# An attention, mixture-of-experts and feed-forward kernel: the second item's expert by signed comparisons, five low parts on GpSimd, and the last tiles' choice between the last attention units

## The chip, the cores and the metric

The kernel runs on one core of one Trainium2 chip. The metric is the device time of one execution in microseconds (us). The kernel before was timed three times: median 835.39 us, from 835.25 to 836.21. Rows of the trace come from one further execution that was profiled; times in them count from the start of its span.

## The reference, cut

```python
# attention: 4 batches x 8 heads, 576 positions, 64 per head; causal window of 128; a slope per head
scores = where(mask, q @ k.T / sqrt(64) + bias, -1e9)
attn = softmax(scores) @ v                         # -> x, 2304 tokens x 512
# mixture of experts: 8 experts, one per token
logits = x @ w_gate + modality_bias[modality_id]
e_idx = argmax(logits, axis=1)
gate_w = softmax(logits)[e_idx]
for e in range(8):
    h = maximum(x[e_idx == e] @ w1[e], 0.0)        # 512 -> 1024
    out[e_idx == e] = gate_w * (h @ w2[e])         # 1024 -> 512
# feed-forward: 512 -> 2048 -> 512, weights in float64
h = out @ w_in
return (h * cos(h)) @ w_out
```

## The kernel before

**Precision.** Products that need all of float32 are made from two parts: a high part, which is the number cast to fp32r, and a low part, which is the number minus its high part. One product of weights and activations is then three matmuls: high by high, high by low, low by high. For a piece of expert weights the raw load lands in `r1` or `r2` (two buffers each, 128x1024 float32), ScalarE (ACT) makes the high part by a cast, and VectorE (DVE) the low part by a subtraction that reads the raw data and the high part. This is `split_w1` (L502) and `split_w2` (L1184). A raw buffer is free for the next load when the low part is done.

**Attention.** 18 tiles of 128 tokens, each in two halves of four heads, make 36 units. A unit n passes `tr` (transposes of q and k, split into parts), `score`, `flip` (transposes of the exponentials, through `pa` and `pT`) and `pv`, which writes its half of a tile `X[t]`; after the second half the tile is stored to `x_dram`. The two last tiles are called `y`.

**Routing.** `xt_split` transposes a finished tile into the two parts `xT`. For each pair of tiles `logits(t)` (L854) gives three calls: `products` (the gate's 8 matmuls and a copy `ls`), `choose` (transposes of `ls`, then 8 small DVE instructions from `lg` to the one-hots `oh` and `ohb`) and `ranks(t)` (L241). `ranks` makes counting products from `ohb`, the running `cum` and constants `tri` and `ones`; folds them into each token's rank in its expert; adds the pair to `cum`; and cuts the rank into blocks of 128 and a remainder, by `ri`, `ph`, `pf` and the one-hots `ob`.

**The order of experts.** Experts have 256 slots per item. The first item's expert is the fullest after the first 12 tiles (`early`, L265); its gathered rows and weights are asked for while the attention still runs. The other eight come from the counts of all 18 tiles (`late`, L320). `sums` turns the counts `rp` into numbers per expert: `K3` (full items, and halves that are over), their prefix sums `pre` over the order of experts `M`, and the block starts `pblk` and `endF`. `slots` makes each token's place as one-hots `oa`, `table` the index table `idx` by products on TensorE, and `experts`, held behind `oa`, the expert of each item: intervals of blocks, folded and cast to `regs`. `load_w1(i, 0)` (L226) reads item i's entry of `regs` on the SP queue and issues the load with it.

**Items.** Nine items of 8 steps each; step f is an up product (12 matmuls `bk<-xT,s`) of item i, and three steps later its down product (12 matmuls `bk<-hh,s`). Weights come in four pieces of W1 and four of W2 per item, W1(i, g) and W2(i, g). Split pieces live in the three tiles `s_0`, `s_1`, `s_2` for W1 (`s1s`) and two more, also printed as `s_0` and `s_1`, for W2 (`s2s`). The first item's up products 0 to 3 run within the attention stage, on two split pieces in a buffer of K that is no longer used (`s1k`, tile name `kT`). `hh` is the rectified result in two parts, made by ACT and DVE; the down sums are evicted to `y` by both. In the loop ACT and DVE also convert the feed-forward's float64 weights, a bit at a time (`from_f64`, L112: `mag`, `top`, `lf`, `wi_a`); the multiplication `lf` of 128x512 is GpSimd's (POOL), and the conversion's loads are on SP between the weight loads.

**What sets the order.** Instructions are put in order by a scheduler, except where a chain is made: `issue_after` puts an instruction behind another on its engine. `Turns` (L523) does so for all instructions of an engine while it is on (for TensorE and POOL nearly all of the attention stage, for ACT and DVE its final sequence: program order there); `InOrder` does the same in steps 12 to 66. `behind("act", "dve")` holds the splits of the first two steps behind marks of the last `xt_split`. The gathers of rows are issued by POOL, the other loads and the stores by SP, in the order of the program's queues.

The final sequence of the attention stage is at L980 to L1017: scores of units 34 and 35, splits of W1(0, 0) and W1(0, 1), `xt_split` of tiles 15, 16 and 17, the calls of `last14` (tiles 14 and 15) and `last16` (16 and 17), and `up_products(0, 0)` to `(0, 3)` between. Its last lines are

```python
        up_products(0, 2)
        last16[1]()
        up_products(0, 3)
        for eng in (nc.scalar, nc.vector, nc.gpsimd, nc.tensor):
            eng.on = False
        after = last16[2:]
```

and what stands in `after`, `ranks(T - 2)`, `sums`, `slots`, `table` and `experts`, is taken up in the loop over steps, one or two calls a step.

Of the kernel before, what the change touches and what calls it, by code (L numbers as in the profile page):

```python
# [29 lines left out]
def kernel(  # L30
# [174 lines left out]
    regs = rt.tile([1, 2 * NL + 2], I32, name="regs")  # L205
    xTs = [rt.tile([128, 2, KD, SLOTS], F32R, name=f"xT{j}") for j in range(2)]
# [15 lines left out]
    W1, HH = {}, {}  # L222
    E = {}
# [17 lines left out]
    def ranks(t):  # L241
# [8 lines left out]
        fold(rank[:, t:t + 2], rp[:, 0:2], oh[:, t:t + 2], [128, 2, NE], rt)  # L250
        if t == 0:
            V_.tensor_tensor(cum, oh[:, 0], oh[:, 1], op=ALU.add)
        elif t + 2 < T:
            V_.tensor_tensor(cum, cum, oh[:, t], op=ALU.add)
            V_.tensor_tensor(cum, cum, oh[:, t + 1], op=ALU.add)
        ri = rt.tile([128, 2], I32, name="ri")
# [5 lines left out]
        one_hot(ob[:, t:t + 2], 128, pf[:, 1, t:t + 2], 2)  # L262

# [56 lines left out]
    def late():  # L320
# [3 lines left out]
        A3 = rt.tile([128, 3, NE], F32, name="A3")  # L324
        a3 = rt.tile([128, 3, T], F32, name="a3")
        pidx = rt.tile([128, NE], F32, name="pidx")
        pblk = rt.tile([128, NE], F32, name="pblk")
        endF = rt.tile([128, NE], F32, name="endF")
# [4 lines left out]
        def sums():  # L333
# [20 lines left out]
            V_.tensor_scalar(A3[:, 0], pre[:, 0], 2.0, None, op0=ALU.mult)  # L354
            V_.tensor_scalar(A3[:, 1], K3[:, 0], 2.0, None, op0=ALU.mult)
            V_.tensor_tensor(endF, A3[:, 0], A3[:, 1], op=ALU.add)
            V_.tensor_tensor(A3[:, 2], pblk, endF, op=ALU.subtract)
            E["m9"] = m9

        def experts():  # L360
# [4 lines left out]
            nb = rt.tile([1, NE], F32, name="nb")  # L365
            V_.scalar_tensor_tensor(nb, K3[0:1, 1], 2.0, K3[0:1, 2], op0=ALU.mult, op1=ALU.add)
            V_.tensor_tensor(nb, nb, pblk[0:1], op=ALU.add)
            b = rt.tile(shp, F32, name="b_", tag="fold3")
            inF = rt.tile(shp, F32, name="inF")
            V_.tensor_tensor(inF, bl, rowp(A3[:, 0]), op=ALU.is_ge)  # L370
# [13 lines left out]
        def slots():  # L384
# [9 lines left out]
            MK["oa"] = V_.tensor_tensor(oa, oa, row.unsqueeze(2).to_broadcast([128, T, NBLK]), op=ALU.mult)  # L394
# [11 lines left out]
        def starts():  # L406
# [15 lines left out]
            V_.scalar_tensor_tensor(dq, A3[:, 2], 128.0, dq, op0=ALU.mult, op1=ALU.add)  # L422
# [15 lines left out]
        def rows_of():  # L438
# [3 lines left out]
            V_.scalar_tensor_tensor(dt, a3[:, 0], 128.0, dt, op0=ALU.mult, op1=ALU.add)  # L442
# [46 lines left out]
    def to_xT(i, j, now=True):  # L489
# [6 lines left out]
        def parts():  # L496
            nc.scalar.copy(xT[:, 0, :, cs], pt)
            nc.vector.tensor_tensor(xT[:, 1, :, cs], pt, xT[:, 0, :, cs].bitcast(F32), op=ALU.subtract)

        return parts() if now else parts  # L500

    def split_w1(i, g, s1=None):  # L502
# [4 lines left out]
        def low():  # L507
            nc.vector.tensor_tensor(s1[:, 1], r1, s1[:, 0].bitcast(F32), op=ALU.subtract)
# [3 lines left out]
    def up_products(i, f):  # L512
        g, j = divmod(f, 2)
        w, xT = W1[i, g], xTs[i % 2]
        if j == 0:
            HH[i, g] = bank("S", [128, 2, SLOTS])
        ph = HH[i, g]
        for kk in range(KD):
# [29 lines left out]
    with ExitStack() as c:  # L548
# [8 lines left out]

        MARK = {}
# [84 lines left out]
        def setup_tables():  # L643
# [35 lines left out]
            return turns + [middle]  # L679
# [164 lines left out]
        def xt_split(t):  # L844
# [9 lines left out]
        def logits(t):  # L854
# [3 lines left out]
            def products():  # L858
                pl = bank("L", [2 * NE, 256])
                for a in range(2):  # L860
                    for kk in range(KD):
                        nc.tensor.matmul(pl, wg[:, kk].rearrange("p a e -> p (a e)"), xT[:, a, kk],
                                         start=kk == 0 and a == 0, stop=kk == KD - 1 and a == 1)
# [676 lines left out]
```

## Time and profile before

| | |
|---|---|
| median of three timed runs | 835.39 us |
| the profiled execution: its own time, its span | 838.82 us, 837.1 us |
| mean granted TensorE clock of it | 0.985 |
| busy: TensorE matmul (PE), weight load (PEld) | 800.7 us (96%), 705.9 us (84%) |
| busy: VectorE (DVE), ScalarE (ACT), GpSimd (POOL) | 615.8 us (74%), 492.2 us (59%), 197.8 us (24%) |

An instruction group in the trace has its line, engine and operation, then what it writes and reads by the program's names; buffer numbers are left out, so that `s` stands for all split pieces and `r` for all raw ones. L535 is the one line on which `Turns` issues, so all of the attention stage and the routing has it; L1168 is that of `InOrder`, for the items and what follows. A bracket at the end of a row gives how long the engine was idle before it and what ended that. The down products of the first item begin at 187.6 us, the nine items and the unit behind them end at some 430 us, and the feed-forward fills the rest.

### The profile page before, as it was taken

Reading aid. Unit: us, or ns where it says so; the run is one execution under the profiler, and the core shown is the slowest. Engines: PE = TensorE matmul, PEld = TensorE weight load, DVE = VectorE, ACT = ScalarE, POOL = GpSimd, SP = SyncE. Lnnn points to the kernel's source line nnn. Section 1 sums busy time; section 2 is a strip of 40 time slices with the busy share of each in tenths; the row PEclk is TensorE's granted clock in tenths of the full one; section 3 lists DMA queues with packets and bytes.
Section 4 is the critical chain, followed back from the end, with each engine's and each line's share of the span. In section 5 each row is a group of like instructions: output and inputs, shape, how many; then the busy total and the mean of one; then the engine's idle time right before and its main releaser. Section 6 shows DMA issues by size and latency. Waiting matters only on the chain. (4 is left out here: it accounts for less than half of the span.)

```text
span 837.1 us, 14764 instructions
## 1 busy us (share of the span) xinstructions
PE 800.7 (96%) x5278; PEld 705.9 (84%) x5278; DVE 615.8 (74%) x1472; ACT 492.2 (59%) x912; POOL 197.8 (24%) x256
## 2 busy tenths in 40 slices
PE   8999999997999999999999999999999999999996
PEld 5888988887989999999978788787788888888995
DVE  4777786778899999995749999896665555555562
ACT  6775776562667766664637676754544555444562
POOL 4755664511022222330001221212222001100100
PEclk9999999999899999999999999999999999999998
DMA  9754531352788889778433231501311001100000
GB/s 165 164 141 117 137 95 33 127 190 87 261 281 265 272 259 301 246 234 310 155 107 96 82 117 60 177 25 64 100 56 58 1 1 38 38 1 1 26 26 25
DMA packets 125134, 103.40 MB, mean 124 GB/s; under 512 B 61725, under 2 KB 105027, under 8 KB 125059
## 3 DMA queue, kind: packets, MB, share of 16 engines
q1 hardware_dynamic: 121043, 92.48, 37.0%
q0 software_dynamic: 2960, 9.70, 3.4%
q8 instruction: 42, 0.69, 0.3%
q10 hardware_dynamic: 1056, 0.26, 0.2%
q14 instruction: 33, 0.27, 0.1%
HBM read 85.90 MB, written 16.52 MB: 122 GB/s over the span
## 5 line engine op out<-in xcount | busy, mean ns | idle before, releaser
L1168 PE MATMUL bk<-hh,s 128*128 128x256 f32 x864 | 118.3, 286 | 6.5 <-DVE y L1168 3.5
L1168 PEld LDWEIGHTS bk<-hh,s 128*128 128x128 f32 x864 | 109.4, 192 | 8.0 <-DVE y L1168 4.3
L1168 PE MATMUL bk<-xT,s 128*128 128x256 f32 x816 | 112.4, 288 | 3.9 <-ACT s L1168 3.5
L1168 POOL TENSOR_TENSOR lf<-lf,mag 128x512 f32<-128x512 f32 x32 | 47.2, 1474 | 287.1 <-DVE mag L1168 261.9
L1168 PEld LDWEIGHTS bk<-xT,s 128*128 128x128 f32 x816 | 105.3, 196 | 4.5 <-ACT s L1168 3.7
L1168 PE MATMUL bk<-yT,wi_a 128*128 128x512 f32 (+1 forms) x480 | 104.1, 368 | 1.2 <-DVE yT L1168 0.8
L1168 PE MATMUL bk<-yT,wi_b 128*128 128x512 f32 (+1 forms) x480 | 104.8, 367 | 0.0
L1168 ACT CAST s<-r 128x1024 fp32r<-128x1024 f32 x70 | 73.0, 1049 | 52.7 <-DMA r<-in_moe_w_dram 33.9
L1168 DVE TENSOR_TENSOR s<-r,s 128x1024 fp32r<-128x1024 f32 x70 | 92.1, 1317 | 15.6 <-ACT s L1168 14.8
L1168 ACT ACTIVATE r<-r 128x512 f32<-128x512 f32 (+1 forms) x80 | 47.2, 590 | 93.6 <-DVE r L1168 93.6
L1168 PEld LDWEIGHTS bk<-yT,wi_a 128*128 128x128 f32 x480 | 83.7, 188 | 17.3 <-DVE yT L1168 1.1
L1168 PEld LDWEIGHTS bk<-yT,wi_b 128*128 128x128 f32 x480 | 84.4, 188 | 15.7
L1168 DVE TENSOR_TENSOR r<-bk,r 128x512 f32<-128x512 f32 (+1 forms) x80 | 51.0, 637 | 61.0 <-ACT r L1168 60.3
L1168 PE MATMUL bk<-wo_b,gg 128*128 128x512 f32 x384 | 93.4, 391 | 1.8 <-DVE po L1168 1.1
L1168 PE MATMUL bk<-wo_a,gg 128*128 128x512 f32 x384 | 92.7, 390 | 0.3 <-DVE gg L1168 0.2
L1168 PEld LDWEIGHTS bk<-wo_b,gg 128*128 128x128 f32 x384 | 71.5, 188 | 18.6 <-issue 1.3
L1168 PEld LDWEIGHTS bk<-wo_a,gg 128*128 128x128 f32 x384 | 71.9, 188 | 16.1 <-DVE gg L1168 1.2
L1168 DVE TENSOR_TENSOR gg<-r,gg 128x512 fp32r<-128x512 f32 x64 | 46.6, 728 | 34.4 <-ACT gg L1168 34.4
L535 PE MATMUL bk<-vt,pT 128*128 128x65 f32 x544 | 65.6, 273 | 0.2 <-POOL pT L535 0.2
L535 PEld LDWEIGHTS bk<-vt,pT 128*128 128x128 f32 x544 | 63.6, 192 | 1.8 <-issue 1.2
L1168 ACT CAST gg<-r 128x512 fp32r<-128x512 f32 x64 | 39.7, 620 | 41.0 <-DVE r L1168 40.9
L1168 DVE SCALAR_TENSOR_TENSOR r<-ki,bk 128x512 f32<-128x512 int32 (+1 forms) x80 | 50.4, 630 | 14.8 <-ACT ki L1168 14.2
(274 smaller groups left out, 1286.7 us busy)
## 6 DMA issues: line engine op xcount, KB each, us to landing
r<-in_moe_w_dram SPq DMA_DIRECT2D x72, 512.0 KB
y_dram<-y SPq DMA_DIRECT2D x19, 256.0 KB
rqk<-in_q_dram SPq DMA_DIRECT2D x32, 128.0 KB
vt<-in_v_dram SPq DMA_DIRECT2D x32, 128.0 KB
x_dram<-xt SPq DMA_DIRECT2D x16, 256.0 KB
f64x<-in_moe_w_in_dram SPq DMA_DIRECT2D x8, 512.0 KB
raw<-in_moe_w_dram SPq DMA_DIRECT2D x8, 512.0 KB
yg<-y_dram SPq DMA_DIRECT2D x16, 256.0 KB
```

The costliest lines, as they stand in the source:

```text
L535: self.last = op(*args, **kwargs)
L1168: r = op(*args, **kwargs)
```

## The change

It does four things.

1. **The second item's expert.** `sums` also computes `nb`, the block where an expert's odd half item ends, and from four borders per expert, compared with 2 and multiplied by constant signs, sums to the number of the expert that holds block 2. That number is cast to a register of its own, `reg1`, which `load_w1(1, 0)` reads. `signed` holds the signs times the expert's number, four small instructions in the attention stage. `A3`, `endF`, `pblk` and `nb` become rows of one tile `Q6`; `experts` still makes the others' entries.
2. **Low parts on GpSimd.** `split_w1` and `split_w2` take an engine. W2(0, 0), W1(0, 2), W2(0, 1), W1(0, 3) get their low part from GpSimd and live in spare buffers of K (`spare`), and W2(0, 2) gets its from GpSimd too, in the loop.
3. **The last four tiles' choice.** `ranks` is cut in `rank_counts` (TensorE), `rank_sums` and `rank_parts` (DVE). Choice and counts of tiles 14 and 15 go between the last attention units, `xt_split` of tiles 16 and 17 and the choice of these move ahead, and their counts stand before `up_products(0, 3)`.
4. **Loads of the first item.** W1(0, 2), W2(0, 1), W1(0, 3) and W2(0, 2) are asked for within the final sequence; in the loop W2 of the first item is asked for before W1 of the second. The loop's splits begin at W1(1, 0) and W2(0, 2), held behind marks of the sequence's last instructions on ACT, DVE and POOL while n is below 8.

```diff
...
     def load_w1(i, g):
         if g == 0:
             rg = 2 * NL + 1 if i == 0 else i
-            EV[i] = nc.sync.value_load(regs[0:1, rg:rg + 1], min_val=0, max_val=NE - 1)
+            EV[i] = nc.sync.value_load(reg1 if i == 1 else regs[0:1, rg:rg + 1], min_val=0, max_val=NE - 1)
...
-            V_.tensor_scalar(A3[:, 0], pre[:, 0], 2.0, None, op0=ALU.mult)
-            V_.tensor_scalar(A3[:, 1], K3[:, 0], 2.0, None, op0=ALU.mult)
-            V_.tensor_tensor(endF, A3[:, 0], A3[:, 1], op=ALU.add)
-            V_.tensor_tensor(A3[:, 2], pblk, endF, op=ALU.subtract)
+            V_.tensor_scalar(A3[:, 2], pre[:, 0], 2.0, None, op0=ALU.mult)
+            V_.tensor_scalar(A3[:, 0], K3[:, 0], 2.0, None, op0=ALU.mult)
+            V_.tensor_tensor(endF, A3[:, 2], A3[:, 0], op=ALU.add)
+            V_.scalar_tensor_tensor(nb, K3[:, 1], 2.0, K3[:, 2], op0=ALU.mult, op1=ALU.add)
+            V_.tensor_tensor(nb, nb, pblk, op=ALU.add)
+            at2 = rt.tile([1, 4, NE], F32, name="at2", tag="fold3")
+            V_.scalar_tensor_tensor(at2, Q6[0:1, 2:6], 2.0, signed, op0=ALU.is_le, op1=ALU.mult)
+            e1 = rt.tile([1, 1], F32, name="e1_")
+            V_.tensor_reduce(e1, at2, op=ALU.add, axis=AX.XY)
+            V_.tensor_copy(reg1, e1)
+            V_.tensor_tensor(A3[:, 1], pblk, endF, op=ALU.subtract)
...
+            def signs():
+                for j in range(4):
+                    nc.vector.tensor_scalar(signed[:, j], iota[0:1, 0:NE], -1.0 if j % 2 else 1.0, None, op0=ALU.mult)
...
-    def split_w1(i, g, s1=None):
+    def split_w1(i, g, s1=None, eng=None):
...
-            nc.vector.tensor_tensor(s1[:, 1], r1, s1[:, 0].bitcast(F32), op=ALU.subtract)
+            (eng or nc.vector).tensor_tensor(s1[:, 1], r1, s1[:, 0].bitcast(F32), op=ALU.subtract)
...
         run(flip(N - 4))
         low()
+        load_w1(0, 2)
+        load_w2(0, 1)
         xt_split(TX - 1)
         half = to_xT(0, 0, False)
         run(flip(N - 3))
         low = split_w1(0, 1, s1k[1])
+        home = spare()
+        split_w2(0, 0, as_w2(home[0]), nc.gpsimd)
         pv(N - 4)
         last14[0]()
         low()
-        half()
-        to_xT(0, 1)
+        load_w1(0, 3)
+        load_w2(0, 2)
+        halves = [half, to_xT(0, 1, False)]
+        halves = [h() for h in halves]
         run(flip(N - 2))
+        last14[1]()
         pv(N - 3)
+        rank_counts(TX - 2)
+        halves[0]()
         run(flip(N - 1))
         pv(N - 2)
-        pv(N - 1)
-        xt_split(T - 2)
-        last14[1]()
+        halves[1]()
+        split_w1(0, 2, as_w1(home[1]), nc.gpsimd)()
+        xt_split(T - 2, lambda: pv(N - 1))
+        xt_split(T - 1)
         up_products(0, 0)
-        xt_split(T - 1)
-        up_products(0, 1)
-        last14[2]()
-        last16[0]()
+        rank_sums(TX - 2)
+        rank_parts(TX - 2)
+        home = spare()
+        last16[0](lambda: split_w2(0, 1, as_w2(home[0]), nc.gpsimd))
+        up_products(0, 1, range(2))
+        last16[1]()
+        up_products(0, 1, range(2, KD))
+        split_w1(0, 3, as_w1(home[1]), nc.gpsimd)()
         up_products(0, 2)
-        last16[1]()
+        rank_counts(T - 2)
         up_products(0, 3)
+        MARK.update(act=nc.scalar.last, dve=nc.vector.last, pool=nc.gpsimd.last)
...
+        def after16():
+            rank_sums(T - 2)
+            rank_parts(T - 2)
+
+        after = [after16]
...
-        done_l = 2
-        done_s = [2, 0]
+        done_l = NF // 2
+        done_s = [NF // 2, 2]
...
-                        low = (split_w1, split_w2)[a](*pieces[done_s[a]])
+                        low = (split_w1, split_w2)[a](*pieces[done_s[a]], None, nc.gpsimd if done_s[a] == 2 else None)
...
         after.pop(0)()
-        with behind("act", "dve"):
-            splits(2, 1)
...
+                    if pieces[done_l - 1][0] == 0:
+                        load_w2(*pieces[done_l - 1])
                     if done_l < len(pieces):
                         load_w1(*pieces[done_l])
-                    if done_l:
+                    if pieces[done_l - 1][0]:
                         load_w2(*pieces[done_l - 1])
                     done_l += 1
-                if n == 1:
-                    splits(3, 2)
...
-                    with behind(*("act", "dve")[:2 if n < 2 else 0]):
+                    with behind("act", "dve", "pool") if n < NF else ExitStack():
                         splits((n + 1) // 2 + 3, n // 2 + 1)
...
```

On GpSimd, at the end of the attention stage, before (`pT` is made by the last attention units, `xg` are gathered rows):

```order
L535 AFFINE_SELECT pT<-pa 128x512 x4
L1168 DMA xg_99<-x_dram,idx 128x512
L1168 DMA xg_100<-x_dram,idx 128x512
L1168 DMA xg_99<-x_dram,idx 128x512
L1168 DMA xg_100<-x_dram,idx 128x512
```

and in the change, from the same place on (`kT` are the spare buffers of K with the first item's pieces, `s_0` is the tile of W2(0, 2)):

```order
L558 AFFINE_SELECT pT<-pa 128x512 x4
L558 TENSOR_TENSOR kT<-r_3124,kT 128x1024
L558 TENSOR_TENSOR kT<-r_3274,kT 128x1024
L558 TENSOR_TENSOR kT<-r_3276,kT 128x1024
L558 TENSOR_TENSOR kT<-r_3330,kT 128x1024
L1227 TENSOR_TENSOR s_0_3552<-r_3332,s_0_3552 128x1024
L1227 DMA xg_101<-x_dram,idx 128x512
```

Five subtractions of 128x1024 stand between the last `pT` and the first gather with the table `idx`.

On DVE, the sums of tiles 14 and 15 up to the first instruction of the choice of tiles 16 and 17, before:

```order
L535 TENSOR_TENSOR fold<-bk,oh 128x16
L1168 TENSOR_TENSOR s_0_3519<-r_3118,s_0_3519 128x1024
L535 TENSOR_REDUCE rank<-fold 128x2
L535 TENSOR_TENSOR cum<-cum,oh 128x8
L1168 TENSOR_TENSOR s_2_3518<-r_3563,s_2_3518 128x1024
L535 TENSOR_TENSOR cum<-cum,oh 128x8
L535 CAST ri<-rank 128x2
L1168 SCALAR_TENSOR_TENSOR hh<-bk,hh 128x512
L535 TENSOR_SCALAR ph<-ri 128x2 x2
L1168 TENSOR_TENSOR s_0_3516<-r_3605,s_0_3516 128x1024
L535 CAST pf<-ph 128x2x2
L535 TENSOR_TENSOR ob<-iota,pf 128x256
```

and in the change:

```order
L558 TENSOR_TENSOR fold<-bk,oh 128x16
L558 TENSOR_REDUCE rank<-fold 128x2
L558 TENSOR_TENSOR cum<-cum,oh 128x8 x2
L558 CAST ri<-rank 128x2
L558 TENSOR_SCALAR ph<-ri 128x2 x2
L558 CAST pf<-ph 128x2x2
L558 TENSOR_TENSOR ob<-iota,pf 128x256
L558 TENSOR_TENSOR lg<-bk,biasm 128x16
```

Three low parts and one `hh` no longer stand among the small instructions.

On TensorE, from the first item's up products to the counts of tiles 16 and 17, before (`xT_97,kT` is up with the pieces in K's buffer, `hh,s_0` is down, `xT_97,s_2` is up(0, 4); `tri` opens the counts):

```order
L535 MATMUL bk<-xT_98,wg 16x256 x8
L535 MATMUL bk<-xT_97,kT 128x256 x12
L535 MATMUL bk<-ident,ls 128x16 x2
L535 MATMUL bk<-xT_97,kT 128x256 x12
L1168 MATMUL bk<-hh,s_0_3519 128x256 x9
L1168 MATMUL bk<-xT_97,s_2_3518 128x256 x12
L1168 MATMUL bk<-hh,s_0_3519 128x256 x4
L1168 LDWEIGHTS tri
L1168 MATMUL bk<-ohb,tri 128x8
```

and in the change (`xT_99,kT` is up):

```order
L558 MATMUL bk<-xT_99,kT 128x256 x12
L558 MATMUL bk<-xT_100,wg 16x256 x8
L558 MATMUL bk<-xT_99,kT 128x256 x6
L558 MATMUL bk<-ident,ls 128x16 x2
L558 MATMUL bk<-xT_99,kT 128x256 x18
L558 LDWEIGHTS tri
L558 MATMUL bk<-ohb,tri 128x8
```

The counts stand 18 up products behind the transposes of `ls`, and up(0, 3) behind the counts.

## Rows read from the trace of the kernel before

**Rows 1.** Waits of TensorE from 170 us on: line, releaser, total us, times, longest.

```profile
PE bk L1168 <- ACT s L1168: 3.5, 1, 3.5
PE bk L1168 <- DVE y L1168: 3.5, 3, 1.4
...
PE bk L1168 <- DMA xg<-x_dram,idx: 1.6, 2, 0.8
...
PE bk L1168 <- DVE s L1168: 0.5, 1, 0.5
```

**Rows 2.** Timeline of TensorE, 185 to 218 us: start, us, instruction, xcount, [idle before <-releaser].

```profile
185.88 0.29 PE L535 MATMUL bk<-ident,ls 16*128 16x16 f32 x2
...
190.58 0.18 PE L1168 MATMUL bk<-ohb,tri 128*128 128x8 bf16 x1
...
209.74 0.79 PE L1168 MATMUL bk<-xT,s 128*128 128x256 f32 x2 [3.48 <-ACT s L1168]
...
215.48 1.58 PE L1168 MATMUL bk<-hh,s 128*128 128x256 f32 x12
216.90 1.60 PE L1168 MATMUL bk<-xT,s 128*128 128x256 f32 x12
```

**Rows 3.** Windows: us, PE PEld DVE ACT POOL busy (xcount), PEclk, DMA share, GB/s.

```profile
206.00:208.00 2.00, 0.26 (x3) 0.03 (x1) 1.09 (x5) 0.81 (x2) 0.98 (x2) 1.00 1.02 353
...
212.00:214.00 2.00, 2.00 (x12) 2.00 (x11) 1.72 (x3) 1.20 (x2) 0.00 (x0) 0.50 1.01 346
214.00:216.00 2.00, 2.00 (x15) 2.00 (x15) 2.00 (x3) 1.31 (x2) 0.00 (x0) 0.75 0.61 164
```

**Rows 4.** Timeline of DVE, 173 to 203 us.

```profile
173.31 1.22 DVE L535 TENSOR_TENSOR kT<-r,kT 128x1024 fp32r<-128x1024 f32 x1
...
190.16 0.17 DVE L535 TENSOR_TENSOR ohb<-rev,lm 128x16 bf16<-128x16 f32 x1
...
198.89 0.65 DVE L535 TENSOR_TENSOR oa<-oa,row 128x468 f16<-128x468 f16 x1
...
202.82 0.17 DVE L535 CAST regs<-ie 1x17 int32<-1x17 f32 x1
```

**Rows 5.** The SP queue's timeline around 203.8 us.

```profile
203.84 0.38 SPq L233 DMA_DIRECT2D r<-in_moe_w_dram  x1
```

**Rows 6.** Timeline of ACT around 170.7 and 208.6 us.

```profile
170.70 1.05 ACT L535 CAST kT<-r 128x1024 fp32r<-128x1024 f32 x1
...
208.64 1.04 ACT L1168 CAST s<-r 128x1024 fp32r<-128x1024 f32 x1 [1.54 <-DMA r<-in_moe_w_dram]
```

**Rows 7.** Timeline of POOL around 103.5 and 236.4 us.

```profile
103.32 0.73 POOL L535 TENSOR_TENSOR kT<-rT,kT 128x256 fp32r<-128x256 f32 x1
104.00 0.76 POOL L535 TENSOR_TENSOR qT<-rT,qT 128x256 fp32r<-128x256 f32 x1
...
236.40 2.11 POOL L1168 TENSOR_TENSOR lf<-lf,mag 128x512 f32<-128x512 f32 x1 [28.91 <-DVE mag L1168]
```

**Rows 8.** Timeline of DVE at the same places, and 10 us later.

```profile
103.45 0.63 DVE L535 TENSOR_TENSOR oh<-rev,lm 128x16 f32<-128x16 f32 x1
...
104.09 0.28 DVE L535 CUSTOM_DVE_ANT_0 sx<-bk,bias 128x128 f32<-128x128 f32 x1
...
237.27 1.78 DVE L1168 TENSOR_TENSOR top<-top,wi_a 128x512 f32<-128x512 f32 x1
...
246.96 0.68 DVE L1168 TENSOR_TENSOR top<-top,wi_a 128x512 f32<-128x512 f32 x1
```

**Rows 9.** Tile lf on POOL: ns min/median/max, first and last start us, forms.

```profile
L1168 POOL TENSOR_TENSOR lf<-lf,mag x32: 1283/1302/2359, 236.4 to 563.2; 128x512 f32<-128x512 f32 x32
```

**Rows 10.** Timeline of DVE, 228 to 236 us.

```profile
228.73 1.23 DVE L1168 TENSOR_TENSOR s<-r,s 128x1024 fp32r<-128x1024 f32 x1 [2.06 <-ACT s L1168]
...
234.66 1.22 DVE L1168 TENSOR_TENSOR s<-r,s 128x1024 fp32r<-128x1024 f32 x1 [0.84 <-ACT s L1168]
```

**Rows 11.** Timeline of TensorE at 248 us.

```profile
248.03 1.41 PE L1168 MATMUL bk<-hh,s 128*128 128x256 f32 x9 [1.38 <-DVE y L1168]
```

More of the change, by code (lines that the diff above doesn't have):

```diff
@@ L205 @@
     regs = rt.tile([1, 2 * NL + 2], I32, name="regs")
+    reg1 = rt.tile([1, 1], I32, name="reg1")
+    signed = rt.tile([1, 4, NE], F32, name="signed")
     xTs = [rt.tile([128, 2, KD, SLOTS], F32R, name=f"xT{j}") for j in range(2)]
@@ L249, in ranks, with rank_sums @@
                 nc.tensor.matmul(rp[:, j], a, b, start=n == 0, stop=n == len(ab) - 1)
-        fold(rank[:, t:t + 2], rp[:, 0:2], oh[:, t:t + 2], [128, 2, NE], rt)
+    def rank_sums(t):
+        fold(rank[:, t:t + 2], E["rp"][:, 0:2], oh[:, t:t + 2], [128, 2, NE], rt)
         if t == 0:
@@ L255, in ranks, with rank_parts @@
             V_.tensor_tensor(cum, cum, oh[:, t + 1], op=ALU.add)
+    def rank_parts(t):
         ri = rt.tile([128, 2], I32, name="ri")
@@ L262, in ranks @@
         one_hot(ob[:, t:t + 2], 128, pf[:, 1, t:t + 2], 2)
+    def ranks(t):
+        rank_counts(t)
+        rank_sums(t)
+        rank_parts(t)
     def early():
@@ L494, in to_xT, with high, low @@
         cs = slice(128 * j, 128 * j + 128)
-        def parts():
+        def high():
             nc.scalar.copy(xT[:, 0, :, cs], pt)
+            return low
+        def low():
             nc.vector.tensor_tensor(xT[:, 1, :, cs], pt, xT[:, 0, :, cs].bitcast(F32), op=ALU.subtract)
-        return parts() if now else parts
-    def split_w1(i, g, s1=None):
+        return high()() if now else high
+    def split_w1(i, g, s1=None, eng=None):
         s1 = W1[i, g] = s1s[(NF // 2 * i + g) % len(s1s)] if s1 is None else s1
@@ L507, in low, with split_w2, up_products @@
         def low():
-            nc.vector.tensor_tensor(s1[:, 1], r1, s1[:, 0].bitcast(F32), op=ALU.subtract)
+            (eng or nc.vector).tensor_tensor(s1[:, 1], r1, s1[:, 0].bitcast(F32), op=ALU.subtract)
         return low
-    def up_products(i, f):
+    def split_w2(i, g, s2=None, eng=None):
+        s2 = W2[i, g] = s2s[(NF // 2 * i + g) % len(s2s)] if s2 is None else s2
+        r2 = R2.pop((i, g))
+        nc.scalar.copy(s2[:, 0], r2)
+        (eng or nc.vector).tensor_tensor(s2[:, 1], r2, s2[:, 0].bitcast(F32), op=ALU.subtract)
+    def up_products(i, f, kks=range(KD)):
         g, j = divmod(f, 2)
         w, xT = W1[i, g], xTs[i % 2]
-        if j == 0:
+        if j == 0 and kks[0] == 0:
             HH[i, g] = bank("S", [128, 2, SLOTS])
         ph = HH[i, g]
-        for kk in range(KD):
+        for kk in kks:
             for a, b in ((0, 0), (0, 1), (1, 0)):
@@ L842, in pv, with xt_split @@
                             later(p + at // 2, at % 2, fn)
-        def xt_split(t):
+        def xt_split(t, between=None):
             xT = xTs[(t // 2 + 1) % 2]
@@ L849, in xt_split @@
                 nc.tensor.transpose(pt[:, kk], X[t][:, 128 * kk:128 * kk + 128], ident)
+            if between:
+                between()
             MARK["act"] = nc.scalar.copy(xT[:, 0, :, c0:c0 + 128], pt)
@@ L856, in logits, with products @@
             ls = rt.tile([2 * NE, 256], F32, name="ls", tag="fold4")
-            def products():
+            def products(between=None):
                 pl = bank("L", [2 * NE, 256])
@@ L863, in products @@
                                          start=kk == 0 and a == 0, stop=kk == KD - 1 and a == 1)
+                if between:
+                    between()
                 nc.scalar.copy(ls, pl)
```

49 lines of the change are left out of this document (22 added, 27 removed).

## Prediction

> **What bounds the kernel now.** I read the waits of TensorE from the end of the attention on first, then its timeline around the longest one, the granted clock there, and last what the other engines did before it. TensorE is busy nearly throughout, so only its few waits can be won. The longest is one of 3.5 us on "ACT s"; 3.5 us in three pieces are on the eviction "DVE y", 1.6 us on gathered rows and 0.5 us on "DVE s" [rows 1]. The 3.5 us stand at 209.74, before the first product of the second item: it waits for the first piece of its weights, then 0.5 us more for that piece's low part [rows 1, 2]. The granted clock falls from 1.00 to 0.50 (1.2 of 2.4 GHz) during that wait and is not whole again before 216 us [rows 3]: the 24 products that start at 209.74 end when the next start, 215.48, so they take 5.2 us besides the 0.5 us of waiting. At full clock twelve take 1.42 us (215.48 to 216.90) [rows 2], so 24 take 2.8 and the clock costs 2.4 us. **The place is worth 8.0 us** (3.5, 0.5, 1.6, 2.4).
>
> What comes before it: the choice of the last two tiles ends at 190.3 on VectorE (DVE), its counting products run at 190.58 on TensorE, and the expert numbers are written at 203.0, after all the routing sums [rows 2, 4]. The load that needs them is issued at 203.84 [rows 5], and ScalarE casts its data at 208.64, when they have landed [rows 6].
>
> **The change, part by part.** All times are on the clock of the profiled run of before. Its own time is 838.82 us (span 837.1 and 1.7 around it), 3.4 us over the median of the three timed runs, 835.39; the difference that I find I carry over to the median.
>
> *The expert by signed comparisons.* The chain to reg1 has the old sums up to the block starts, then comparisons, one sum and one cast, and no longer the table's one-hots and all the sums behind them. Counts to old register were 12.4 us (190.58 to 203.0). To the end of the one-hots, 199.5 [rows 4], they were 9.0; I subtract a low part (1.15), the steps between reg1 and that end (2.1), and add the five new small steps (0.45) and a wait for hh (0.4): 6.6 us from counts to reg1. Taken alone the load is 5 to 6 us earlier. The four sign rows lie in the attention stage, some 0.15 us each on an engine with gaps there: nothing.
>
> *The low parts on GpSimd.* Five subtractions leave DVE, 1.22 us each [rows 4], 5.7 us together as neighbours overlap by some 0.09. No row shows GpSimd doing one of 128x1024. It takes 0.73 us for 128x256 [rows 7] and 1.30 for 128x512 [rows 9], so I estimate 2.45 on that line; the ends are 2.2 (three times 0.73) and 2.6 (twice 1.30). That is 12.2 us on an engine idle from 172 to 200 us, and free only if DVE does not notice.
>
> It notices. While GpSimd ran kT<-rT,kT from 103.32 for 0.73 us [rows 7], a DVE instruction on 16 elements that reads two SBUF tiles (like the ohb of 0.17 us [rows 4]) took 0.63 and ended with GpSimd's [rows 8]. At 236.40 GpSimd itself waited for DVE's low part and took 2.11, and the DVE subtraction behind took 1.78 where its like takes 0.68 [rows 7, 8]. Beside GpSimd's next instruction, from 104.00, one with an input in PSUM ran its 0.28 us [rows 7, 8]. So one waits out the other. The Trainium skill says this too: in "SBUF — State Buffer", section "SBUF: two separate sides", the shared port pair is held for the whole instruction, and a DVE instruction in a 2-port mode or with two SBUF inputs blocks fully. The trace agrees as far as it goes (holds of some 0.5 to 1.1 us); no row has a hold of 2.45 us. By the rule every hold here is as long as the instruction; if none passed what is seen, the time would be that of B2 below.
>
> Where that falls:
> 1. ScalarE casts W1(0,1) from 170.70 for 1.05 us [rows 6] and then W2(0,0), to 172.7. GpSimd starts at 172.8 and ends at 175.25. DVE's own low part, at 173.31 [rows 4], is **held 1.9 us**. The choice of tiles 14 and 15 now follows it and ends at 177.8; its counts, moved ahead on TensorE, wait 1.7 us.
> 2. TensorE then does what it did before, in another order, and ends up(0,2) 1.7 us later than the 185.9 of before [rows 2], at 187.6.
> 3. ScalarE's casts let GpSimd do W1(0,2) at 180.3, harmlessly (DVE reads PSUM then), W2(0,1) at 183.9, W1(0,3) at 186.3 and W2(0,2) at 188.75, end to end until 191.2.
> 4. At 183.5 DVE begins rank_sums and rank_parts, of which the second cum, ph, pf and ob each wait for the one before and may not run beside GpSimd. Each seam between two GpSimd instructions lets one link through: three holds, **6.8 us**. The choice of tiles 16 and 17 begins at 191.7 and ends at 193.2, not 190.3.
> 5. Its counts stand on TensorE before up(0,3) now, no longer behind 25 products of down and up. TensorE waits from 187.6 to 193.3, **5.7 us**, and as in the old wait the clock falls: another 2.4 us.
> 6. reg1 comes 6.6 us after the counts, at 199.9, 3.1 us before the old register. The load is issued 0.85 us later and castable 4.8 us after that, as before [rows 5, 6], at 205.5; TensorE gets there at 211 or later. The 3.5 and 0.5 us go. So do the 1.6: the gathered rows are now asked for 43 products behind the table, not 26, 2 us more.
>
> *The choice of the last tiles between the units* adds no TensorE work: the same products in another order; its gain is void by 1 and 4. On SP the x_dram stores and two conversion loads stand behind the load of W2(0,2), which waits for GpSimd until 175.25, before the last y exists: nothing. The gathers stand behind GpSimd's five instructions, which end at 191.2, long before their index: nothing.
>
> **The sum.** TensorE: 8.0 us won, 1.7, 5.7 and 2.4 lost, so 1.8 us later in the second item. DVE: minus 5.7, plus 0.45, plus 8.7 held, so 3.4 later, of which 0.4 is lost in gaps that it had before. It is the later of the two, so TensorE waits for its evictions and its one-hots at the first item's end: **3.0 us late**. From there to some 320 us DVE is nearly full and sets the pace, so what counts is its idle time. Before, it idled 2.06 and 0.84 us for casts that waited for data, and smaller gaps lay beside [rows 10]. In the new order two pieces are loaded ahead of the conversion load that delayed them, and a DVE that comes later finds its data: 2.9 us back, and some 0.4 more where the eviction's wait of 1.38 us [rows 11] shrinks because TensorE comes later. Sum: 3.0 minus 3.3, **0.3 us faster: 835.1 us**, which no measurement of this kernel tells from no change (it can tell about 0.2%, 1.7 us).
>
> **The rivals.**
> B1, the holds don't bite (GpSimd's instructions fall between DVE's): counts at 186, all 8.0 us won, DVE 5.2 us ahead (5.7 less 0.45), 2.9 more where it idled; 5 to 8 us, say 7.5: 828. Against it: ScalarE's casts are done before GpSimd wants them, so its instructions touch, and touching ones hold a chain. Chance 0.14.
> B2, the holds are half as long: 3.4 us less wait for the counts and 1 us less of low clock, 4.4 better than the forecast: 831. Chance 0.22.
> C, slower: the lag stays. DVE is 3.0 us late at the first item's end and still idles for data there, since each load waits for a low part that is late too: 838.4. It decides if DVE idles over 2 us between 220 and 240 us. For it: the loop from low part to load to cast is unchanged. Against: the 2.06 us came from one load that stood behind others. That the early number wins nothing, because the load is late for another reason, ends here too. Chance 0.26.
>
> **How the numbers follow.** The forecast, 833.7 to 836.9, has 0.38. Faster by over 0.2% is B1 and B2, 0.36; same 0.38; slower is C, 0.26. The range for 8 in 10 goes from 829, leaving out most of B1, to 839, leaving out a lag larger than C's. GpSimd's 2.2 and 2.6 us (three holds: 0.75 less or 0.45 more) lie inside the forecast's own range.
>
> **What would show it.** Right: GpSimd subtractions of about 2.45 us, three of them end to end; cum, ph or pf of over 2 us on DVE; a wait of TensorE of 5 to 6 us before the second counts with the granted clock at 0.50 behind it; no wait on "ACT s" at the first product of the second item. Wrong: those small instructions at their usual 0.16 us beside GpSimd, or counts before 188 us (then B1 or B2), or a DVE that idles for data at the first item's end (then C).

## The result and the profile after

The changed kernel took 847.92 us (median of 4, 846.77 to 848.56), the kernel before on the same chip 835.80 (835.25 to 838.77): ratio 1.0115, 95% interval 1.0083 to 1.0147. It is **12 us slower**, and the range ended at 839. The profiled execution has a span of 846.5 us (before 837.1), TensorE busy 803.4 us, DVE 616.6, GpSimd 213.1, and a mean granted clock of 0.979.

The waits of TensorE from 165 us on, longest in total first (line, releaser, total us, times, longest), to be read against [rows 1]:

```profile
PE bk L1227 <- DMA xg<-x_dram,idx: 6.3, 1, 6.3
PE bk L558 <- DVE ohb L558: 4.7, 2, 3.5
PE bk L1227 <- DVE y L1227: 4.2, 4, 1.7
```

The waits for "ACT s" and "DVE s" are gone, as forecast. In their place stand one of 6.3 us for gathered rows, which was forecast to go, and two for the one-hots `ohb`. The timeline of TensorE at the three places:

```profile
175.95 0.19 PE L558 MATMUL bk<-ohb,tri 128*128 128x8 bf16 x1 [1.23 <-DVE ohb L558]
...
193.52 0.19 PE L558 MATMUL bk<-ohb,tri 128*128 128x8 bf16 x1 [3.48 <-DVE ohb L558]
...
209.88 0.60 PE L1227 MATMUL bk<-ident,xg 128*128 128x128 f32 x4
216.82 1.08 PE L1227 MATMUL bk<-ident,xg 128*128 128x128 f32 x4 [6.34 <-DMA xg<-x_dram,idx]
```

and its windows (us, PE PEld DVE ACT POOL busy, granted clock, DMA share, GB/s):

```profile
174.00:176.00 2.00, 0.77 (x9) 0.63 (x8) 1.76 (x10) 0.00 (x0) 0.00 (x0) 0.97 0.18 21
176.00:186.00 10.00, 9.50 (x52) 8.82 (x53) 6.25 (x16) 3.65 (x5) 3.76 (x2) 0.50 0.63 203
...
194.00:200.00 6.00, 6.00 (x30) 6.00 (x31) 5.55 (x40) 0.60 (x1) 0.00 (x0) 0.52 0.00 0
...
216.00:220.00 4.00, 3.18 (x15) 3.21 (x16) 1.38 (x3) 1.53 (x2) 0.94 (x1) 0.50 0.13 41
```

Behind each wait the clock is at 0.50 (1.2 of 2.4 GHz): ten us behind a wait of 1.23, six behind 3.48, four behind 6.34. At half clock a stretch does half its work (twelve up products take 2.7 us from 193.76 on, and 1.4 from 205.57 on at full clock), so these cost some 5, 3 and 2 us besides the 11 of waiting. That is an estimate from the windows.

Why the rows come late is seen on three queues. GpSimd:

```profile
171.03 2.37 POOL L558 TENSOR_TENSOR kT<-r,kT 128x1024 fp32r<-128x1024 f32 x1 [0.68 <-ACT kT L558]
...
188.26 2.38 POOL L558 TENSOR_TENSOR kT<-r,kT 128x1024 fp32r<-128x1024 f32 x1 [1.27 <-ACT kT L558]
190.60 2.34 POOL L1227 TENSOR_TENSOR s<-r,s 128x1024 fp32r<-128x1024 f32 x1
205.34 0.96 POOL L1227 DMA_INDIRECT xg<-x_dram,idx  x1 [12.40 <-DVE nu L558]
206.61 4.50 POOL L1227 DMA_INDIRECT xg<-x_dram,idx  x1 [0.30 <-issue]
```

DVE:

```profile
171.56 2.92 DVE L558 TENSOR_TENSOR kT<-r,kT 128x1024 fp32r<-128x1024 f32 x1
...
184.50 2.50 DVE L558 TENSOR_TENSOR cum<-cum,oh 128x8 bf16<-128x8 bf16 x2
...
188.56 2.11 DVE L558 TENSOR_TENSOR lgs<-lg,lmx 128x16 f32<-128x16 f32 x1
190.71 2.26 DVE L558 SCALAR_TENSOR_TENSOR oh<-lgs,rev 128x16 f32<-128x16 f32 x1
...
206.39 1.21 DVE L1227 TENSOR_TENSOR s<-r,s 128x1024 fp32r<-128x1024 f32 x1
...
207.74 1.21 DVE L1227 TENSOR_TENSOR s<-r,s 128x1024 fp32r<-128x1024 f32 x1
...
209.08 1.20 DVE L1227 TENSOR_TENSOR s<-r,s 128x1024 fp32r<-128x1024 f32 x1
```

and SP:

```profile
208.97 0.37 SPq L235 DMA_DIRECT2D r<-in_moe_w_dram  x1
209.59 0.53 SPq L240 DMA_DIRECT2D r<-in_moe_w_dram  x1
210.37 0.37 SPq L235 DMA_DIRECT2D r<-in_moe_w_dram  x1
```

GpSimd's subtractions hold small DVE instructions (`cum`, two of 8 elements, 2.5 us together; `lgs` and `oh`, 16 elements, 2.1 and 2.3 us), as forecast. Later the roles are reversed: three DVE low parts run almost end to end from 206.39 to 210.28, and GpSimd's second gather, issued at 206.61, takes 4.50 us instead of 0.96 and ends 0.8 us after the last of them. Each low part also frees a raw buffer, so three loads of 512 KB are issued at 208.97 to 210.37, ahead of the gather's end at 211.11; its rows are used at 216.82.

### The profile page after: what moved, and what is told of

Same layout as the page of the kernel before. It is cut to its first block, busy times and chain, and to the rows that moved or that the text cites. A ratio compares the mean times of both kernels' runs of the same rounds, so it can differ in the third digit from the quotient of the medians.

```text
span 846.5 us, 14754 instructions
## 1 busy us (share of the span) xinstructions
PE 803.4 (95%) x5278; PEld 709.2 (84%) x5278; DVE 616.6 (73%) x1474; ACT 491.4 (58%) x912; POOL 213.1 (25%) x261
## 5 line engine op out<-in xcount | busy, mean ns | idle before, releaser
L1227 PE MATMUL bk<-hh,s 128*128 128x256 f32 x816 | 113.3, 288 | 6.9 <-DVE y L1227 4.2
L1227 PEld LDWEIGHTS bk<-hh,s 128*128 128x128 f32 x816 | 104.6, 193 | 8.6 <-DVE y L1227 5.3
L1227 PE MATMUL bk<-xT,s 128*128 128x256 f32 x768 | 101.2, 280 | 0.0
L1227 ACT CAST s<-r 128x1024 fp32r<-128x1024 f32 x66 | 69.1, 1050 | 53.1 <-DMA r<-in_moe_w_dram 40.2
L1227 DVE TENSOR_TENSOR s<-r,s 128x1024 fp32r<-128x1024 f32 x65 | 87.0, 1340 | 16.9 <-ACT s L1227 16.4
L1227 PEld LDWEIGHTS bk<-xT,s 128*128 128x128 f32 x768 | 95.2, 188 | 0.0
L558 PE MATMUL bk<-vt,pT 128*128 128x65 f32 x544 | 67.3, 277 | 0.2 <-POOL pT L558 0.2
L558 PEld LDWEIGHTS bk<-vt,pT 128*128 128x128 f32 x544 | 65.3, 196 | 1.8 <-issue 1.2
```

Of the source, the lines that this page charges most:

```text
L558: self.last = op(*args, **kwargs)
L1227: r = op(*args, **kwargs)
```

## The experiments

Each run was timed beside the kernel before on the same chip, where that had medians of 836.1 to 838.4; so ratios count, each with its 95% interval. The quoted text ahead of each result is what was expected of the run, with its rival theories ('holds', 'pace' and so on).

**The gather freed (e2), and its loads put behind it (e13).** (e1 and so on are the runs' names in short.) In e2 three low parts stand on DVE behind the last instruction of `starts`, `dq`:

```diff
+            MK["dq"] = E["dq_ins"]
...
-                        splits((n + 1) // 2 + 3, n // 2 + 1)
+                        if n >= NF - 2:
+                            later.enter_context(tc.issue_after(MK["dq"].ins))
+                            splits((n + 1) // 2 + 3, n // 2 + 1)
+                        else:
+                            splits(4, min(3, n // 2 + 1))
```

> The change with the low parts of W2(0, 3), W1(1, 0) and W1(1, 1) held behind the last starts on VectorE, so that they no longer run beside the second gather, which took 4.5 us there. Theory 'gather' (VectorE's three low parts hold GpSimd's gather of the second half, its rows land 10 us after issue, and TensorE's 6.3 us wait and the half clock behind it come from that): the gather takes about 1 us, the wait falls under 2 us, 840 to 842. Theory 'pace': the low parts come later on a full engine, 846 to 849. Theory 'late loads' (the gather lands late because three weight loads of 512 KB stand ahead of it on the DMA engines, not because it was issued late): the wait shrinks by at most 3 us, 844 to 846.

840.16 us, ratio 1.0031 (1.0002 to 1.0061), from 1.0115. GpSimd's queue and TensorE's transposes in e2:

```profile
208.12 1.00 POOL L1228 DMA_INDIRECT xg<-x_dram,idx  x1 [0.30 <-issue]
```

```profile
211.38 1.04 PE L1228 MATMUL bk<-ident,xg 128*128 128x128 f32 x8
```

The gather takes 1.00 us and the wait is nil. e13 leaves the hold and puts the loads behind it:

```diff
+        if (i, g) == (1, 2):
+            EV[i] = nc.sync.value_load(regs[0:1, i:i + 1], min_val=0, max_val=NE - 1)
```

> The change, where W1(1, 2) and all loads behind it go by the number read again from the table of experts, so that they are issued behind the held gather and not ahead of it; the low parts stay where they hold it. Theory 'hold and loads' (3.5 us of the late rows come from the hold of the gather, some 3 from three weight loads that pass it meanwhile): the gather still takes 4.5 us, TensorE's 6.3 us wait falls to 3 to 4, 844 to 846. Theory 'hold alone': the wait stays over 5.5 us, 847 to 849.

841.85 us, ratio 1.0030 (1.0000 to 1.0060). The gather still takes 4.50 us; TensorE's wait in e13 is halved:

```profile
213.25 1.09 PE L1229 MATMUL bk<-ident,xg 128*128 128x128 f32 x4 [3.23 <-DMA xg<-x_dram,idx]
```

So the hold alone leaves 3.2 of the 6.3 us, and the loads that pass the held gather make the other 3.1. The time is below both ranges that were expected, and the ratio is that of e2, where no wait is left: what the remaining 3.2 us cost does not show in the time, or it lies within the intervals. In e2 the loads are behind the gather too (211.93 us and later), so it does not part the hold from the loads; e13 does.

**Low parts on DVE (e1), and both edits (e5).** The engine argument `nc.gpsimd` is left out at its five places; e5 has e2's edit too.

> The change with its five low parts back on VectorE; all else as in the change. Theory 'holds' (GpSimd's subtractions lock VectorE out, so the choices come late, TensorE waits 1.2 and 3.5 us for the two sets of counts and runs at half clock for 10 and 6 us behind them): both waits shrink to under 1.5 us together, the low clock behind them goes, the late gather stays: 839 to 842 us. Theory 'order' (counts that stand ahead of the up products wait in any case, whoever makes the low parts): both waits stay, 846 to 850. Theory 'pace' (VectorE is the limit from here to 380 us, so only its work counts): 5.7 us more work on it, 848 to 853.

851.73 us, ratio 1.0196 (1.0131 to 1.0262): slower than the change (the intervals just overlap), in the range of 'pace', and 10 us above that of 'holds'. The waits for `ohb` fall from 4.7 to 0.9 us, so the holds did cause those, but in the waits of TensorE in e1 stand

```profile
PE bk L1227 <- DMA xg<-x_dram,idx: 7.3, 2, 5.1
PE bk L1227 <- DVE rhs L558: 5.1, 1, 5.1
```

The gather is held as before (4.05 us), and DVE, with five more low parts, is late with `rhs`, the last routing part.

> Both edits together: the change's five low parts on VectorE, and the low parts of W2(0, 3), W1(1, 0), W1(1, 1) held behind the starts. Theory 'two causes' (holds by GpSimd cost some 5 us before 195 us, the held gather some 7 behind 205; each alone was hidden by a later wait): 832 to 837. Theory 'pace' (VectorE has 5.7 us more to do and sets the time): 840 to 846, with a wait of TensorE for rhs or y in place of the others.

843.81 us, 1.0080 (1.0054 to 1.0106). The second gather takes 0.95 us (the first 1.99), `rhs` is waited for by 4.6 us: the range of 'pace', and 0.5% above e2. With the gather free, GpSimd looks the better place for the five, holds and all; the two intervals just touch.

**The low parts on GpSimd in the kernel before (e8).**

```diff
-                        low = (split_w1, split_w2)[a](*pieces[done_s[a]])
+                        low = (split_w1, split_w2)[a](*pieces[done_s[a]], eng=nc.gpsimd if done_s[a] < 4 - a else None)
```

> The kernel before with nothing but the low parts of W2(0, 0), W1(0, 2), W2(0, 1), W1(0, 3) and W2(0, 2) on GpSimd, each where its cast stands in the loop. Theory 'holds': single VectorE instructions of the routing take over 2 us beside them, the choice of tiles 16 and 17 and the second item's register come 3 to 6 us later, 838 to 842. Theory 'free engine' (5.7 us less on VectorE win more than the holds lose): 830 to 834.

842.93 us, 1.0041 (1.0013 to 1.0068), 0.9 us above the range of 'holds'. On DVE in e8:

```profile
181.84 2.20 DVE L535 TENSOR_TENSOR lgs<-lg,lmx 128x16 f32<-128x16 f32 x1
184.08 2.27 DVE L535 SCALAR_TENSOR_TENSOR oh<-lgs,rev 128x16 f32<-128x16 f32 x1
```

TensorE waits 5.1 us for this `ohb`: 'holds' here too, though it is the choice of tiles 14 and 15 that is held most, not that of 16 and 17.

**The early number alone (e3), with later loads (e6), with a later end of the routing (e7).** e3 is the kernel before with `reg1`; e6 adds

```diff
+        if (i, g) == (1, 1):
+            EV[i] = nc.sync.value_load(regs[0:1, i:i + 1], min_val=0, max_val=NE - 1)
```

and e7 to that `if n == NF:` for `if n == NF - 2:` ahead of `after += l2`.

> The kernel before with the second item's expert by signed comparisons alone. Theory 'early number' (the 3.5 us wait for W1(1, 0), the 0.5 for its low part and 2.4 of low clock go, as the prediction had it): 829 to 832. Theory 'gather' (with the weights early, their low parts run beside the gathers, hold them, and TensorE waits for the rows instead): 834 to 838, with a gather of over 2 us. Theory 'pace': 835 to 836, the wait goes and comes back later as waits for evictions.

841.43 us, 1.0074 (1.0039 to 1.0110): slower, above all three ranges, and not by a held gather. Its gathers take 0.95 and 1.05 us, but the early number lets four loads go at 196.64 to 198.67 on SP, ahead of gathers at 199.15 and 200.40. TensorE in e3:

```profile
206.24 1.11 PE L1177 MATMUL bk<-ident,xg 128*128 128x128 f32 x4 [4.70 <-DMA xg<-x_dram,idx]
...
227.99 0.97 PE L1177 MATMUL bk<-rhs,ob 128*128 128x54 f16 x18 [6.61 <-DVE rhs L540]
```

> The kernel before with the signed comparisons, where only W1(1, 0) and the W2(0, 3) behind it go by the early number; from W1(1, 1) on the number is read again from the table of experts, so that the other loads are issued behind the gathers as before. Theory 'late loads' (with the early number alone, four loads of 512 KB stood ahead of the gathers on the DMA engines and their rows came at 206 instead of 203 us): TensorE's 4.7 us wait for rows falls under 1.5, 833 to 837 with the wait for rhs still there, 829 to 832 if that goes too. Theory 'pace': 838 to 842, as the early number alone.

837.79 us, 0.9988 (0.9956 to 1.0019). The wait for rows falls from 4.7 to 1.0 us, as 'late loads' has it; the one for `rhs` is 7.3. The time is just above the 833 to 837 that it gives with that wait.

> As the run before, with the last routing part (starts, gates, rows, the products with rhs) called two steps later. Theory 'rhs' (TensorE comes to the products with rhs earlier than VectorE has made them, behind low parts that the scheduler put ahead): the wait for rhs, 6.6 us with the early number alone, falls under 1, 829 to 833. Theory 'pace': the wait only moves, within 1.5 us of the run before.

839.83 us, 1.0036 (1.0000 to 1.0072). In e7 TensorE makes the transposes of the second rows at 204.05 (the kernel before at 205.63) and has no wait of 3.5 us behind them, but this one:

```profile
226.24 0.97 PE L1179 MATMUL bk<-rhs,ob 128*128 128x54 f16 x18 [8.66 <-DVE rhs L542]
```

Calling the part later made DVE later, not TensorE's wait shorter: the wait moved, as 'pace' has it, though the time is 2 us above e6 and not within 1.5. In the kernel before the same products start at 220.23 without a wait: there DVE makes four low parts between the last routing register (`regs`) and `rhs`, in e7 six. The lead of 1.6 us at the second rows does not come from e7's edits: this execution was 1.8 us ahead at 168 us already.

**The counts of tiles 16 and 17 later (e4).** `rank_counts(T - 2)` moves from ahead of `up_products(0, 3)` into `after16`.

> The change with the counts of tiles 16 and 17 taken out of the order ahead of up(0, 3) and left to the scheduler behind it. Theory 'holds': TensorE does up(0, 3) within the 3.5 us wait, but then lacks hh, which stands behind the choice on VectorE, and the chain to the gather still begins at the choice: 845 to 847. Theory 'order' (the place of the counts is what cost): 840 to 843.

845.89 us, 1.0116 (1.0065 to 1.0167): in the range of 'holds'; the place of the counts is not what cost. Up to there e4 is the change, and its profiled execution has the same first wait, but not the fall of the clock behind it:

```profile
177.57 0.18 PE L558 MATMUL bk<-ohb,tri 128*128 128x8 bf16 x1 [1.23 <-DVE ohb L558]
```

```profile
176.00:178.00 2.00, 0.77 (x14) 0.64 (x13) 1.73 (x12) 0.00 (x0) 0.00 (x0) 1.00 0.32 84
178.00:188.00 10.00, 9.31 (x77) 8.43 (x76) 8.76 (x17) 6.83 (x10) 6.67 (x3) 1.00 0.83 257
```

So the fall behind this wait is not in every execution.

**GpSimd's instructions in quarters (e9), two fewer on GpSimd (e10), quarters with later counts (e11),** all on e2:

```diff
+            for k in range(KD) if eng else [slice(0, KD)]:
+                (eng or nc.vector).tensor_tensor(s1[:, 1, k], r1[:, k], s1[:, 0, k].bitcast(F32), op=ALU.subtract)
```

> The change with the three low parts behind the starts (as the run with the gather freed) and each of GpSimd's five subtractions cut into four of 128x256. Theory 'holds' (a VectorE instruction with two SBUF inputs waits out the one GpSimd instruction that runs, so a quarter of the length holds a quarter as long): no routing instruction over 1 us beside them, the choice of tiles 16 and 17 ends 2 to 3 us earlier, TensorE's 3.5 us wait for it falls under 1.5, 836 to 839. Theory 'queue' (VectorE is slow there whatever GpSimd's pieces are): 839 to 842 and the same wait.

837.57 us, 0.9991 (0.9966 to 1.0017). On DVE in e9 the instructions that took 2.11 and 2.26 us read

```profile
194.49 0.62 DVE L561 TENSOR_TENSOR lgs<-lg,lmx 128x16 f32<-128x16 f32 x1
195.14 0.67 DVE L561 SCALAR_TENSOR_TENSOR oh<-lgs,rev 128x16 f32<-128x16 f32 x1
```

and the wait for `ohb` is 0.5 us: 'holds'. Yet TensorE's windows in this execution of e9 are

```profile
170.00:172.00 2.00, 1.37 (x9) 0.99 (x9) 0.75 (x2) 1.66 (x4) 1.37 (x3) 1.00 0.31 69
172.00:174.00 2.00, 2.00 (x13) 2.00 (x13) 0.00 (x0) 1.68 (x2) 1.32 (x3) 0.59 1.07 396
174.00:182.00 8.00, 8.00 (x46) 7.14 (x46) 3.87 (x13) 2.01 (x4) 3.54 (x4) 0.50 0.43 148
182.00:192.00 10.00, 9.50 (x45) 8.69 (x45) 6.54 (x20) 3.64 (x5) 4.55 (x7) 0.50 0.37 110
```

half clock for 20 us from 172 on, behind a wait of 0.97 us for `pa`. The kernel before has the same wait, and its profiled execution keeps the clock there. All profiled runs have it but the two with filled waits below; the clock falls behind it in e5, e6, e9, e10, e15 and e17, for 3 to 20 us, and stays at 1.00 in the others. The span of this execution of e9 is 843.7; the ten executions go from 834.1 to 845.5.

> The run with the gather freed, and W1(0, 3) and W2(0, 2) back on VectorE behind the choice; W2(0, 0), W1(0, 2), W2(0, 1) stay on GpSimd. Theory 'holds': the choice of tiles 16 and 17 runs free and ends at 190 instead of 194.8 us, the 3.5 us wait goes, 835 to 838. Theory 'pace': 2.4 us more work on VectorE, the products with rhs wait 3 us or more, 840 to 843.

839.91 us, 1.0020 (0.9982 to 1.0057), between the two theories: the wait for `ohb` goes (0.6), one of 2.6 us for `rhs` comes.

> Quarters as above, and the counts of tiles 16 and 17 behind up(0, 3). Theory 'holds': what is left of the wait for the choice is covered by up(0, 3), 1.4 us, with the half clock behind it: 1 to 3 us under the quarters alone, 833 to 837. Theory 'pace': no difference from the quarters alone within 1 us, the time comes back as a wait for rhs or y.

838.19 us, 1.0000 (0.9974 to 1.0026): no gain on e9. 'holds' misses; 'pace' has it, within 1 us of e9 and with waits of 2.6 us for `rhs` and 3.9 for y.

**The conversions spread over 50 steps (e14 to e17),** `N1 - C0 - 2` for `N1 - C0 - 6`, on the kernel before, e6, e9 and e11:

> The kernel before with the conversion of the feed-forward's first weights spread over 50 steps instead of 46, some 7 us of VectorE's work moved from between 220 and 370 us to behind. Theory 'pace': TensorE's waits for y (3.5 us) and the idle of the routing shrink, 1 to 3 us faster than before. Theory 'latency' (the waits come from single late pieces, VectorE's load does not matter): within 0.5 us of before, or slower where the late conversions stand in the way at the items' end.

837.42 us, 0.9993 (0.9966 to 1.0019): no difference that can be told.

> The early number with the other loads behind the gathers (837.8 us, 0.9988 of before) and the conversions spread. Theory 'pace': more of the lead of 4.8 us at 215 us is kept, 2 to 4 us faster than before. Theory 'rhs' (the lead is lost at the products with rhs, before the conversions begin in earnest): within 1 us of what it was.

840.00 us, 1.0027 (1.0001 to 1.0053) against e6's 0.9988, `rhs` 6.7 us.

> The change with the gather freed and GpSimd's low parts in quarters (837.6 us, 0.9991 of before), with the conversions spread. Theory 'pace': 2 to 4 us faster than before. Theory 'rhs': within 1 us of what it was.

841.21 us, 1.0033 (1.0005 to 1.0060) against e9's 0.9991, but from 834.5 to 844.2, and the execution that was profiled, clock whole to 192 us, has a span of 833.2.

> Gather freed, quarters, counts behind up(0, 3) (838.2 us, 1.000 of before), with the conversions spread. Theory 'pace': 2 to 4 us faster than before. Theory 'rhs': within 1 us of what it was.

843.48 us, 1.0050 (1.0023 to 1.0077) against e11's 1.0000. Theory 'pace' falls in this form: four times its 1 to 4 us did not come. 'rhs' is not met either: e15, e16 and e17 came out 0.4 to 0.5% slower, for e16 and e17 by more than the intervals allow. Why is not shown.

**The waits filled (e18, e19).** On e16, idle matmuls in three waits; on the kernel before in the first alone:

```diff
+        def fill(n):
+            b = bank("O", [128, 512])
+            for _ in range(n):
+                nc.tensor.matmul(b, still[:, 0:128], still, start=True, stop=True)
...
+        fill(4)
         run(flip(N - 3))
...
+        fill(4)
         rank_counts(TX - 2)
...
+        fill(6)
         rank_counts(T - 2)
```

> The run with quarters and spread conversions (841.2 us, from 834.5 to 844.2), with matmuls on a constant tile, whose result nobody reads, in TensorE's waits: 4 of 512 columns ahead of the transposes that wait for pa, 4 ahead of the counts of tiles 14 and 15, 6 ahead of those of 16 and 17. Theory 'clock' (half clock behind these waits makes the slow executions): the granted clock stays whole to 200 us in all but few, median 834 to 837, faster than before by 1 to 4. Theory 'other' (the spread has another cause): median 839 to 843, the same spread.

**833.14 us** (831.27 to 837.68), ratio **0.9956** (0.9933 to 0.9979) to the kernel before on the same chip: faster than both kernels, 0.9 us under the range of 'clock', and by the ratios some 6.5 us under e16 by this edit alone, with a third less spread. TensorE's windows in e18:

```profile
168.00:172.00 4.00, 3.80 (x32) 3.26 (x31) 1.76 (x5) 2.86 (x5) 3.13 (x6) 1.00 0.75 266
172.00:176.00 4.00, 4.00 (x39) 3.28 (x38) 3.73 (x12) 1.59 (x4) 2.86 (x3) 1.00 0.47 133
176.00:192.00 16.00, 15.31 (x127) 13.70 (x126) 14.45 (x50) 8.40 (x12) 11.42 (x16) 1.00 0.55 164
```

The mean granted clock that is listed for every execution says the same. In e16 the seven above 841 us have 0.978 to 0.984 and the five below 839 have 0.986 to 0.992; in e18 all twelve have 0.989 or more. The change itself was not run with its waits filled.

> The kernel before with 4 matmuls of 512 columns on a constant tile ahead of the transposes that wait for pa, at 168 us. Theory 'clock': its slower executions (over 839) go, median 834 to 837. Theory 'other': median 837 to 839 with the same spread.

838.10 us, 0.9996 (0.9969 to 1.0024), from 835.6 to 841.7: no gain. The kernel before does not lose its clock there but behind the 3.5 us wait, which stayed.

## Why the prediction was wrong

*The expert by signed comparisons.* Right. The register was forecast for 199.9 and written at 199.79 (a cast of 0.13 us at 199.66), the load issued at 200.61 against 203.84 [rows 5], the data cast at 204.33 against 208.64 [rows 6]; the waits for "ACT s" and "DVE s" went. What that is worth alone was not: e3 is slower than the kernel before.

*The low parts on GpSimd.* Right in size: 2.34 to 2.39 us against 2.45, `ohb` ready for counts at 193.52 against 193.3, the first hold 1.7 us (2.92 less 1.22) against 1.9. Three more holds followed, as forecast, but their places were right only in part: one fell on `cum`, the other two on `lgs` and `oh` of the choice itself, and none on `ph`, `pf` or `ob`; two of GpSimd's instructions stood end to end and not three. e9 shows the mechanism: a quarter of the length, under a third of the held time.

*TensorE's wait for the second counts.* 3.48 us against 5.7, because TensorE came late itself. The first wait, 1.23 us, was forecast at 1.7 without a fall of the clock; in the profiled execution it cost ten us at half clock, 5 us. e16 against e18 shows that the clock behind such short waits decides several us, and e4 and e9 that it falls in some executions and not in others.

*The step that failed* is in point 6, "So do the 1.6", with the sentence on SP and the gathers, "nothing". For the first gather it held: its rows are used at 209.88 without a wait. For the second it failed. GpSimd was free long before the index, but at the gather DVE held it, and in the 3.5 us of the hold weight loads passed it. The rows, waited for by 1.6 us before, were waited for by 6.3, with some 2 us of half clock behind. The loads put behind the gather (e13) or the hold removed as well (e2) both bring the ratio from 1.0115 to 1.003: some 7 of the 12 us, give or take 4 by the intervals. The prediction had the rule for the pair, "one waits out the other", and used it in one direction. The trace shows the other: 4.50 us beside three low parts and 0.96 to 1.00 without. The Trainium skill has something near it in the section that the prediction draws on ("SBUF — State Buffer", "SBUF: two separate sides"): a DMA that GpSimd issues has its descriptors written by GpSimd, which a DVE instruction in a 2-port mode locks out. The trace agrees only so far: the low parts are subtractions with two inputs in SBUF, and no run shows them in such a mode.

*The other 5 us.* Two terms stood at nothing in the sum, the second rows (6.3 us of waiting and 2 of clock) and the clock behind the first wait (5 us); they make some 13 of the 21 us that TensorE lost to waits and clock, where 9.8 were forecast (1.7, 5.7 and 2.4). What the second term is worth in the median was not measured on the change. With the gather free and GpSimd's instructions in quarters (e9) the ratio is 0.9991, so the rest of the loss may go with the holds by GpSimd; the intervals hardly tell e9 from e2 (1.0031). The 8.0 us that the prediction wins do not show even there.

*The sum* is read where both kernels have done the same products to within four, at the transposes of the third item's first rows. Before:

```profile
224.72 0.60 PE L1168 MATMUL bk<-ident,xg 128*128 128x128 f32 x4
```

and after:

```profile
235.86 0.62 PE L1227 MATMUL bk<-ident,xg 128*128 128x128 f32 x4
```

TensorE is 11.1 us late there, not 3.0; 9.4 are left in the span of the profiled executions, so some 1.7 came back and not 3.3.

*The rivals.* B1 and B2 fall with the holds of 1.7 to 2.2 us. C had the sign, and DVE idled behind casts, by 1.84 us at 224.30 and 1.13 at 238.94:

```profile
224.30 1.23 DVE L1227 TENSOR_TENSOR s<-r,s 128x1024 fp32r<-128x1024 f32 x1 [1.84 <-ACT s L1227]
...
238.94 1.23 DVE L1227 TENSOR_TENSOR s<-r,s 128x1024 fp32r<-128x1024 f32 x1 [1.13 <-ACT s L1227]
```

But on ACT these casts waited for TensorE, and not for loads as C has it:

```profile
223.22 1.05 ACT L1227 CAST s<-r 128x1024 fp32r<-128x1024 f32 x1 [1.93 <-PE bk L1227]
...
237.87 1.05 ACT L1227 CAST s<-r 128x1024 fp32r<-128x1024 f32 x1 [0.77 <-PE bk L1227]
```

So the trace does not bear out C's mechanism, its sign came out by another path, and its price, 3 us, is the smaller part of 12.

*Left open:* what limits the kernels in which TensorE leads at 215 us. `rhs` takes the lead where the low parts go ahead of it on DVE (e3, e6, e7, e15), but spreading the conversions won nothing, and an order in which DVE makes `rhs` first was not tried.

## What to carry to other kernels

When work moves between VectorE and GpSimd, look at both directions of the hold, and at every gather that GpSimd issues: a chain of large VectorE instructions beside it delays its rows by the chain. A load that can start earlier starts ahead of something; look at what it passes on the DMA engines before counting its gain. A wait of 1 us on TensorE can cost 5 by the clock in one execution and nothing in the next, so price waits with the clock behind them, and try idle matmuls in them: they won in e18 and not in e19.

## What the runs showed that was not expected

Three DVE subtractions with only small instructions between them held one gather over all three: 4.50 us against 0.96. The clock fell to 0.50 behind waits of 1.23 us and, in e9, of 0.97 us, and stayed there for 10 and 20 us while TensorE was busy 9.5 of 10; in other executions it did not fall behind the same waits. Fourteen idle matmuls in such waits took the ratio to the kernel before from 1.0033 to 0.9956.
